# Linear attention into a SwiGLU block: turning phi(q) by 128x128 transposes instead of making phi on turned q, for one batch

## Chip, cores, metric

One core of a Trainium2 chip. The metric is the device time of one run in microseconds (us). "The stage" is a stretch from the first layer-2 matmul of the first token group to the first matmul of line L292 in the second group (its third block of layer 1; the first two blocks are line L276): it holds everything that the change touches.

## The reference, cut to what matters

```python
def phi(x):
    return np.where(x > 0, x, np.exp(x) - 1.0) + 1.0
q_p, k_p = phi(q), phi(k)                      # (8, 8, 576, 64)
kv  = einsum('bhsd,bhse->bhde', k_p, v)        # 64x64 per head
z   = k_p.sum(axis=2)
out = einsum('bhsd,bhde->bhse', q_p, kv) / (einsum('bhsd,bhd->bhs', q_p, z) + 1e-6)
x   = out, tokens x (heads*64)                 # 4608 x 512
y   = (silu(x @ w_gate) * (x @ w_val)) @ w_out # d_ff = 1536
```

With fp16 data the kernel computes phi as max(x, 0) + min(exp(x), 1), which is the same function.

## The kernel before: the parts concerned

The work goes in nine groups of 512 tokens. Per group, layer 1 is 12 blocks of 8 matmuls, layer 2 is 48 matmuls of 512 columns. The attention of the next tokens is woven in between. q and k lie with tokens on the partitions; the attention matmuls need phi(q) with the feature on the partitions, so q must be turned. For batch 1 this is done inside layer 2 of group 0:

```python
def qtr(b, lp, ps):                    # 16 transposes of 64 columns, raw q
    pt = ps[:, :].bitcast(FP16).rearrange("p (j c) -> p j c", c=P)
    for j in range(J - 1):
        for l2 in range(2):
            nc.tensor.transpose(out=pt[D * l2:D * l2 + D, j, :], in_=qr[b][:, 2 * lp + l2, D * j:D * j + D],
                                identity=id16[:, :])
# ... qtr8: 8 more, for column block 8 of batches 0 and 1
def t_phi(a, ps):                      # phi on turned q, out of PSUM
    return (lambda: act(a, ps, AF.Exp),
            lambda: nc.vector.tensor_scalar(out=a, in0=a, scalar1=1.0, scalar2=None, op0=ALU.min),
            lambda: nc.vector.scalar_tensor_tensor(out=a, in0=ps, scalar=0.0, in1=a, op0=ALU.max, op1=ALU.add))
# ...
    step = {1: [s0], 4: [s1, s3], 5: [s5]}    # what is done before which layer-2 block
    FO = 9
    for fb in range(FO):
        for f in step.get(fb, []):
            f()
        for t in range(4):
            l2_mm(0, t, fb)
    s4()                                      # the denominators of group 1
# ... three more blocks, numerators, then layer 1 of group 1
```

## Time and profile before

| | before |
|---|---|
| device time, median of 3 | 315.97 us (315.6 to 316.2) |
| span of the profiled run | 314.1 us |
| TensorE busy | 307.5 us, 98% |
| the stage | 36.75 to 54.88 us: 18.13 us |
| in it, to the first denominator matmul | 9.48 us |

The views used are the page (busy shares, chain that ended last), the chain in order of time (start, length, engine, tile, line), the waits (who waited for whom: total, times, longest), groups of instructions by form (busy time and mean ns, then idle time before them), and the timeline (start, length, engine, line, operation, count). On the timeline a length includes the last matmul's own 0.2 to 0.4 us; to get a pace one subtracts that. PE is TensorE, PEld its weight loads, DVE VectorE, ACT ScalarE, POOL GpSimd. The form of a matmul is the label that the views print behind it: 128*128 for layer 2 and the full-width transposes, 128*64 for the half-width ones, 64*64 for the denominators; a change of form is the step from one label to another.

### The profile page before, as it was taken

Reading aid. Unit: us, or ns where it says so; the run is one execution under the profiler, and the core shown is the slowest. Engines: PE = TensorE matmul, PEld = TensorE weight load, DVE = VectorE, ACT = ScalarE, POOL = GpSimd, SP = SyncE. Lnnn points to the kernel's source line nnn. Section 1 sums busy time; section 2 is a strip of 40 time slices with the busy share of each in tenths; the row PEclk is TensorE's granted clock in tenths of the full one; section 3 lists DMA queues with packets and bytes.
Section 4 is the critical chain, followed back from the end, with each engine's and each line's share of the span. In section 5 each row is a group of like instructions: output and inputs, shape, how many; then the busy total and the mean of one; then the engine's idle time right before and its main releaser. Section 6 shows DMA issues by size and latency. Waiting matters only on the chain.

```text
span 314.1 us, 5531 instructions
## 1 busy us (share of the span) xinstructions
PE 307.5 (98%) x2186; PEld 142.7 (45%) x2186; DVE 205.5 (65%) x362; ACT 152.0 (48%) x231; POOL 48.0 (15%) x72
## 2 busy tenths in 40 slices
PE   8899999999999999999999999999999999999994
PEld 4444444444544454445444544444444444444442
DVE  4854688899789767977597849874991434133410
ACT  4865839738643745366535743475330333133311
POOL 7755334300000230023000500000000000000000
PEclk9999999999999999999999999999999999999999
DMA  8999999995612396129702990314032400140014
GB/s 216 198 198 199 206 207 232 238 206 88 140 33 41 50 180 170 38 41 163 197 20 57 134 230 0 75 35 102 0 61 59 91 1 1 37 98 0 2 33 100
DMA packets 41162, 32.80 MB, mean 104 GB/s; under 512 B 16432, under 2 KB 36144, under 8 KB 41136
## 3 DMA queue, kind: packets, MB, share of 16 engines
q0 software_dynamic: 20464, 18.29, 37.2%
q1 hardware_dynamic: 20592, 14.13, 18.6%
q8 instruction: 17, 0.28, 0.4%
q14 instruction: 9, 0.07, 0.1%
q10 hardware_dynamic: 80, 0.03, 0.0%
HBM read 37.75 MB, written 9.44 MB: 150 GB/s over the span
## 4 chain that ended last, share of the span: by engine, by line
PE 96%; DMA 1%; DVE 1%; ACT 1%; issue 0%
PE pp L292 57%; PE pp L299 30%; PE pp L276 2%; PE pp L254 2%; PE pp L185 2%; DMA q<-in_q_dram 1%; PE pp L124 1%; PE pp L430 1%; ACT qT L120 0%; ACT ek L120 0%; PE pp L371 0%; PE pp L396 0%; DVE kp L159 0%; PE pp L212 0%; DVE ek L147 0%; DVE osb L322 0%
## 5 line engine op out<-in xcount | busy, mean ns | idle before, releaser
L120 ACT ACTIVATE sil<-pp 128x512 f16<-128x512 f32 x108 | 63.4, 597 | 101.8 <-PE pp L292 100.9
L292 PE MATMUL pp<-xT,wg 128*128 128x512 f16 x416 | 106.8, 379 | 0.0
L292 PE MATMUL pp<-xT,wv 128*128 128x512 f16 x416 | 106.8, 379 | 0.0
L285 DVE SCALAR_TENSOR_TENSOR hT<-pp,sil 128x512 f16<-128x512 f32 x108 | 72.4, 682 | 49.0 <-PE pp L292 35.6
L299 PE MATMUL pp<-wo,hT 128*128 128x512 f16 (+2 forms) x444 | 97.2, 374 | 0.6 <-DVE osb L322 0.6
L299 PEld LDWEIGHTS <-hT 128*128 128x128 f16 x444 | 41.9, 98 | 49.7 <-issue 2.1
L292 PEld LDWEIGHTS <-wv 128*128 128x128 f16 x416 | 40.7, 98 | 49.1
L292 PEld LDWEIGHTS <-wg 128*128 128x128 f16 x416 | 40.7, 98 | 48.4
L322 DVE TENSOR_SCALAR osb<-pp 128x512 f32<-128x512 f32 (+1 forms) x19 | 12.9, 682 | 30.6 <-PE pp L299 26.2
L120 ACT ACTIVATE osb<-pp 128x512 f32<-128x512 f32 (+1 forms) x18 | 10.3, 573 | 34.8 <-PE pp L299 34.8
L120 ACT ACTIVATE ek<-kr 128x1152 f16<-128x1152 f16 x16 | 17.8, 1156 | 0.1
L120 ACT ACT_TABLE_LOAD x13 | 16.7, 1283 | 2.3 <-PE pp L292 2.1
L693 POOL COPY gate<-qT 128x1 f16<-128x1 f16 x4 | 1.3, 320 | 97.9 <-DVE hT L285 71.2
L229 DVE TENSOR_TENSOR qp<-qp,rden 128x1152 f16<-128x1152 f16 x12 | 16.2, 1347 | 0.0
L220 DVE TENSOR_REDUCE den<-prod 128x18 f32<-128x1152 f16 x12 | 16.1, 1344 | 0.0
L271 DVE TENSOR_SCALAR xT<-pp 128x512 f16<-128x512 f32 (+1 forms) x14 | 8.8, 667 | 7.1 <-PE pp L254 7.1
L120 ACT ACTIVATE eq<-qr 128x1152 f16<-128x1152 f16 x12 | 13.2, 1147 | 0.0
L103 POOL DMA_DIRECT2D vr<-in_v_dram x16 | 11.7, 735 | 9.3 <-PE pp L292 3.5
L103 POOL DMA_DIRECT2D kr<-in_k_dram x16 | 11.7, 735 | 7.8 <-DMA wo<-in_moe_w_out_dram 1.8
L147 DVE TENSOR_SCALAR ek<-ek 128x1152 f16<-128x1152 f16 x16 | 7.7, 483 | 7.5 <-ACT ek L120 7.5
L159 DVE TENSOR_TENSOR kp<-ek,kp 128x1152 f16<-128x1152 f16 x16 | 12.1, 758 | 0.5
L103 POOL DMA_DIRECT2D qr<-in_q_dram x14 | 10.1, 723 | 5.8 <-DMA wo<-in_moe_w_out_dram 1.8
(76 smaller groups left out, 183.6 us busy)
## 6 DMA issues: line engine op xcount, KB each, us to landing
out_dram<-osb SPq DMA_DIRECT2D x70, 128.0 KB, 3.2
kr<-in_k_dram POOLq DMA_DIRECT2D x16, 288.0 KB, 8.9
vr<-in_v_dram POOLq DMA_DIRECT2D x16, 288.0 KB, 9.8
qr<-in_q_dram POOLq DMA_DIRECT2D x14, 288.0 KB, 12.1
wo<-in_moe_w_out_dram POOLq DMA_DIRECT2D x3, 512.0 KB, 12.7
wg<-in_moe_w_gate_dram POOLq DMA_DIRECT2D x5, 256.0 KB, 9.1
wv<-in_moe_w_val_dram POOLq DMA_DIRECT2D x5, 256.0 KB, 9.7
q<-in_q_dram SPq DMA_DIRECT2D x2, 576.0 KB, 4.1
```

The lines of the kernel that those rows point to most:

```text
L103: nc.gpsimd.dma_start(out=dst[b % NB][:, 2 * lp:2 * lp + 2, :], in_=src[b].rearrange("(l a) (c j) d -> (a c) l (j d)", a=2, j=J)[:, 2 * lp ...
L120: nc.scalar.activation(out=out, in_=in_, func=func, bias=bias, scale=scale)
L147: nc.vector.tensor_scalar(out=a, in0=a, scalar1=1.0, scalar2=None, op0=ALU.min)
L159: nc.vector.tensor_tensor(out=a, in0=ek[b % 2][:, lp, :, :], in1=a, op=ALU.add)
L185: nc.tensor.matmul(out=ps[hh][D * l2:D * l2 + D, D * lp:D * lp + D], lhsT=t[b % 2][rows, lp, j, D * l2:D * l2 + D], rhs=vr[b % NB][rows, 2 ...
L220: nc.vector.tensor_reduce(out=den[:, c, :], in_=prod[:, :, :].rearrange("p j (l d) -> p (j l) d", d=D), axis=AX.X, op=ALU.add)
L229: nc.vector.tensor_tensor(out=qv, in0=qv, in1=rden[:, c, :].unsqueeze(2).to_broadcast([P, 2 * J, D]), op=ALU.mult)
L271: nc.vector.tensor_scalar(out=dst, in0=ps[l2][:, c0:], scalar1=1.0 / SC, scalar2=None, op0=ALU.mult)
L285: nc.vector.scalar_tensor_tensor(out=hT[g % 2][:, fb, :], in0=ps[1][:, :], scalar=SC, in1=s[:, :], op0=ALU.mult, op1=ALU.mult)
L292: nc.tensor.matmul(out=ps[h][:, :], lhsT=w[:, c, P * fb:P * fb + P], rhs=xT[g % 2][:, c, :], start=(c == 0), stop=(c == 3))
L299: nc.tensor.matmul(out=l2p[(g, t)][:, n0:n1], lhsT=hT[g % 2][:, fb, P * t:P * t + P], rhs=wo[:, fb, n0:n1], start=(fb == 0), stop=(fb == F ...
L322: nc.vector.tensor_scalar(out=o[:, n0:n1], in0=ps[:, n0:n1], scalar1=1.0 / SC, scalar2=None, op0=ALU.mult)
```

## The change

Its intent is to halve the transposes (20 full-width ones in place of 40 half-width ones), and to take phi's work on PSUM off VectorE: phi(q) is made in the given layout out of SBUF, turned, and copied by ScalarE. To give VectorE room, half of the z sum goes to TensorE as nine 2-column matmuls.

```diff
-    def qtr(b, lp, ps):
+    def turn(lp, ps):
         pt = ps[:, :].bitcast(FP16).rearrange("p (j c) -> p j c", c=P)
         for j in range(J - 1):
-            for l2 in range(2):
-                nc.tensor.transpose(out=pt[D * l2:D * l2 + D, j, :], in_=qr[b][:, 2 * lp + l2, D * j:D * j + D],
-                                    identity=id16[:, :])
+            nc.tensor.transpose(out=pt[:, j, :], in_=qp[1][:, lp, j, :], identity=id16[:, :])
+        act(qT[1][:, lp, 0:8, :, :].rearrange("p j h c -> p (j h c)"), ps[:, :].bitcast(FP16))
 # ... mx_p, add_p: max and add of phi in the given layout; phi_q8: the same for block 8 of batch 0
 # ... turn8, copy8: block 8, one transpose per half, copied by VectorE
     def p1_z():
-        for lp in range(2):
-            ps = b1p["z"][1]
-            nc.tensor.matmul(out=ps[:, 2 * lp:2 * lp + 2], lhsT=zs[:, lp, 0, :], rhs=ob[:, 0:P:C],
-                             start=True, stop=True)
+        ps = b1p["z"][1]
+        nc.tensor.matmul(out=ps[:, 0:2], lhsT=zs[:, 0, 0, :], rhs=ob[:, 0:P:C], start=True, stop=True)
+        for j in range(J):
+            nc.tensor.matmul(out=ps[:, 2:4], lhsT=kp[1][:, 1, j, :], rhs=ob[:, 0:P:C],
+                             start=(j == 0), stop=(j == J - 1))
 # ...
         def s0():
-            qtr(1, 0, cq[0])
+            act(eq[0][:, :, D * 8:D * 9], qr[0][:, :, D * 8:D * 9], AF.Exp)
             exp_k(1, 1)
-            pm[0][0]()
+            exp_q(1, 0)
+            exp_q(1, 1)
+            phi_q8()
+            mx_p(0)
             mn_k(1, 1)
             add_k(1, 1)
-            zsum(1, 1, 2)
 # ...
+            mn_q(1, 0)
+            add_p(0)
+            mx_p(1)
+            mn_q(1, 1)
+            add_p(1)
         def s1():
# ... the old bodies of s1, s3 and s5 are left out
+            turn(0, cq[0])
         def s3():
+            turn(1, cq[1])
+            for b in range(2):
+                for lp in range(2):
+                    turn8(b, lp, dz[0])
             p1_z()
+            for b in range(2):
+                copy8(b, dz[0])
-        step = {1: [s0], 4: [s1, s3], 5: [s5]}
+        step = {1: [s0], 6: [s1], 8: [s3]}
```

More of the change, by code (lines that the diff above doesn't have):

```diff
@@ L363 @@
         nc.vector.memset(ob[C * h:C * h + C, C * h:C * h + C], 1.0)
-    def qtr(b, lp, ps):
+    def turn(lp, ps):
         pt = ps[:, :].bitcast(FP16).rearrange("p (j c) -> p j c", c=P)
         for j in range(J - 1):
-            for l2 in range(2):
-                nc.tensor.transpose(out=pt[D * l2:D * l2 + D, j, :], in_=qr[b][:, 2 * lp + l2, D * j:D * j + D],
-                                    identity=id16[:, :])
-    def qtr8(ps):
-        pt = ps[:, :].bitcast(FP16).rearrange("p (b i c) -> p b i c", i=4, c=P)
-        for b in range(2):
-            for lp in range(2):
-                for l2 in range(2):
-                    nc.tensor.transpose(out=pt[D * l2:D * l2 + D, b, lp, :],
-                                        in_=qr[b][:, 2 * lp + l2, D * 8:D * 9], identity=id16[:, :])
@@ L382, in t_phi @@
-    def t_phi(a, ps):
-        return (lambda: act(a, ps, AF.Exp),
-                lambda: nc.vector.tensor_scalar(out=a, in0=a, scalar1=1.0, scalar2=None, op0=ALU.min),
-                lambda: nc.vector.scalar_tensor_tensor(out=a, in0=ps, scalar=0.0, in1=a, op0=ALU.max, op1=ALU.add))
-    def t_phi_main(b, lp, ps):
-        return t_phi(qT[b][:, lp, 0:8, :, :].rearrange("p j h c -> p (j h c)"), ps[:, :].bitcast(FP16))
-    def t_phi_8(b, ps):
-        return t_phi(qT[b][:, :, 8, :, :].rearrange("p l h c -> p l (h c)"),
-                     ps[:, 256 * b:256 * b + P].bitcast(FP16).rearrange("p (l c) -> p l c", l=2))
+            nc.tensor.transpose(out=pt[:, j, :], in_=qp[1][:, lp, j, :], identity=id16[:, :])
@@ new lines, in turn, with mx_p, add_p, turn8 @@
+        act(qT[1][:, lp, 0:8, :, :].rearrange("p j h c -> p (j h c)"), ps[:, :].bitcast(FP16))
+    def mx_p(lp):
+        nc.vector.tensor_scalar(out=jl(qp, 1, lp), in0=lj(qr, 1, lp), scalar1=0.0, scalar2=None, op0=ALU.max)
+    def add_p(lp):
+        nc.vector.tensor_tensor(out=jl(qp, 1, lp), in0=jl(qp, 1, lp),
+                                in1=eq[1][:, hs(lp), :].rearrange("p l (j d) -> p l j d", d=D), op=ALU.add)
+    def turn8(b, lp, ps):
+        pt = ps[:, :].bitcast(FP16).rearrange("p (b i c) -> p b i c", i=4, c=P)
+        nc.tensor.transpose(out=pt[:, b, lp, :], in_=qp[b][:, lp, 8, :], identity=id16[:, :])
@@ new lines, in copy8, with phi_q8 @@
+    def copy8(b, ps):
+        nc.vector.tensor_copy(out=qT[b][:, :, 8, :, :].rearrange("p l h c -> p l (h c)"),
+                              in_=ps[:, 256 * b:256 * b + P].bitcast(FP16).rearrange("p (l c) -> p l c", l=2))
+    def phi_q8():
+        r, e = qr[0][:, :, D * 8:D * 9], eq[0][:, :, D * 8:D * 9]
+        nc.vector.tensor_scalar(out=r, in0=r, scalar1=0.0, scalar2=None, op0=ALU.max)
+        nc.vector.tensor_scalar(out=e, in0=e, scalar1=1.0, scalar2=None, op0=ALU.min)
+        nc.vector.tensor_tensor(out=qp[0][:, :, 8, :].rearrange("p a (l d) -> p a l d", d=D),
+                                in0=e.rearrange("p (a l) d -> p a l d", l=2),
+                                in1=r.rearrange("p (a l) d -> p a l d", l=2), op=ALU.add)
@@ L524, in p1_z @@
     def p1_z():
-        for lp in range(2):
-            ps = b1p["z"][1]
-            nc.tensor.matmul(out=ps[:, 2 * lp:2 * lp + 2], lhsT=zs[:, lp, 0, :], rhs=ob[:, 0:P:C],
-                             start=True, stop=True)
+        ps = b1p["z"][1]
[3 more added lines that the diff above has]
+                             start=(j == 0), stop=(j == J - 1))
         nc.vector.tensor_scalar(out=Zr[1][:, :, :, :].rearrange("p l h e -> p (l h) e"),
@@ L580, in layer2_0 @@
         cq, dz = b1p["q"], b1p["z"]
-        p8 = [t_phi_8(b, dz[0]) for b in range(2)]
-        pm = [t_phi_main(1, lp, cq[lp]) for lp in range(2)]
         nc.scalar.preload_act_table_set("natural_log_exp_and_others")
@@ L593, in s0 @@
         def s0():
-            qtr(1, 0, cq[0])
+            act(eq[0][:, :, D * 8:D * 9], qr[0][:, :, D * 8:D * 9], AF.Exp)
             exp_k(1, 1)
-            pm[0][0]()
+            exp_q(1, 0)
+            exp_q(1, 1)
+            phi_q8()
+            mx_p(0)
             mn_k(1, 1)
             add_k(1, 1)
-            zsum(1, 1, 2)
-            pm[0][1]()
-            pm[0][2]()
+            mn_q(1, 0)
[3 more added lines that the diff above has]
+            add_p(1)
         def s1():
-            qtr8(dz[0])
-            for f in (0, 1, 2):
-                for b in range(2):
-                    p8[b][f]()
+            turn(0, cq[0])
         def s3():
-            qtr(1, 1, cq[1])
-            pm[1][0]()
-        def s5():
+            turn(1, cq[1])
+            for b in range(2):
+                for lp in range(2):
+                    turn8(b, lp, dz[0])
             p1_z()
-            pm[1][1]()
-            pm[1][2]()
+            for b in range(2):
+                copy8(b, dz[0])
         def s4():
```

## The prediction

> **What bounds the kernel now.** I read the page of the kernel before from the top: busy shares first, then the 40 slices (the granted TensorE clock is 9 tenths or more in all of them, so nothing is to be won by warming), then the chain that ended last.
>
> ```profile
> PE 307.5 (98%) x2186; PEld 142.7 (45%) x2186; DVE 205.5 (65%) x362; ACT 152.0 (48%) x231; POOL 48.0 (15%) x72
> ...
> PE 96%; DMA 1%; DVE 1%; ACT 1%; issue 0%
> ```
>
> TensorE sets the end. Only 6.6 us of the 314.1 us span have no matmul in them, so removed VectorE or ScalarE work is worth nothing unless TensorE waited for it. The change touches only batch 1, whose preparation is woven into layer 2 of the first group. So I next read the chain in order of time there (columns: start, length, engine, tile, source line, count):
>
> ```profile
> 36.91 0.86 PE pp L299 x4
> 37.77 0.57 PE pp L371 x16
> 38.34 2.70 PE pp L299 x12
> 41.04 0.34 PE pp L379 x8
> 41.38 0.45 PE pp L371 x16
> 41.83 0.97 PE pp L299 x4
> 42.80 0.03 PE pp L527 x2
> 42.83 3.48 PE pp L299 x16
> 46.30 0.69 PE pp L254 x16
> ```
>
> The chain never leaves TensorE here. L299 is layer 2, L371 and L379 are the 40 transposes of raw q, L527 sums z, L254 is where the denominators start. From 36.91 to 46.30 is 9.39 us. Layer 2 at its usual pace takes 36 x 0.2155 = 7.76 us (0.2155: sixteen in 3.48 us less the switch, and 96 in 20.72 us elsewhere). The other 1.63 us is everything the change can touch on TensorE. The wait view of that stretch shows what stood idle:
>
> ```profile
> ACT lnt L120 <- PE pp L254: 3.7, 1, 3.7
> ...
> ACT qT L120 <- PE pp L379: 1.4, 1, 1.4
> ```
>
> ScalarE waits for TensorE, never the reverse; it has over 5 us to spare before the denominators. VectorE is busy 8.1 of 9.4 us in that stretch, with little spare. The groups by form give the durations that I use:
>
> ```profile
> L120 ACT ACTIVATE eq<-qr 128x1152 f16<-128x1152 f16 x2 | 2.2, 1147 | 0.0
> L385 DVE SCALAR_TENSOR_TENSOR qT<-pp,qT 128x1024 f16<-128x1024 f16 x2 | 2.5, 1225 | 0.1
> L159 DVE TENSOR_TENSOR kp<-ek,kp 128x1152 f16<-128x1152 f16 x3 | 2.3, 759 | 0.1
> L147 DVE TENSOR_SCALAR ek<-ek 128x1152 f16<-128x1152 f16 x3 | 1.4, 454 | 1.0 <-ACT ek L120 1.0
> L120 ACT ACTIVATE qT<-pp 128x1024 f16<-128x1024 f16 x2 | 2.0, 1018 | 0.0
> L371 PE MATMUL pp<-id,qr 128*64 128x128 f16 x32 | 1.3, 220 | 0.0
> L529 DVE TENSOR_SCALAR Zr<-pp 128x256 f16<-128x256 f32 x1 | 0.4, 416 | 0.0
> ```
>
> [...] nine 2-column matmuls for z early on (0.38 us for nine, of which 0.166 is one matmul's own length) step at (0.38 - 0.17)/8 = 27 ns. [...] the old transposes have the form 128*64, [...]and sixteen take 0.64 us of which 0.22 is one, so they step at 0.42/15 = 28 ns[...]; and the surrounding pieces are longer than their counts by about 0.11 us at each change of form (2.70 us against 12 x 0.2155 = 2.59; 0.97 against 0.86; 0.57 against 16 x 0.028 = 0.45; 0.34 against 0.22). [...] here a copy from PSUM of 1024 should thus cost as exp did, 1018 ns.
>
> **The change, part by part.**
> TensorE. Removed: 40 half-width transposes at 28 ns (1.12 us), four changes of form (4 x 0.115 = 0.46 us), two z matmuls (0.05 us): 1.63 us, the whole of the remainder above. Added: [...]no change of form, since layer 2 is 128*128 too, and ten z matmuls at 28 ns (0.28 us): 1.40 us. Halving the count of transposes thus saves nothing in streaming: the old ones ran in pairs. Net -0.23 us, from switches saved less z moved in.
>
> VectorE. Removed: two min of 1024 (0.52 each), two max-add from PSUM (1.23 each), their small forms (2 x 0.22, 2 x 0.42), and one z sum of four steps (0.43+0.29+0.22+0.22 = 1.16): 5.9 us. Added: two max (0.45), two min (0.45), two add (0.76), the three small ones for column block 8 of batch 0 (0.22+0.22+0.29), two copies from PSUM of 256 (0.42 each, estimated as like the 416 ns row): 4.9 us. One us less, but it isn't on the path.
>
> ScalarE. Removed: exp on PSUM, 2 x 1.02 + 2 x 0.38 = 2.8 us. Added: exp of 2 x 1.15 + 0.42, copies 2 x 1.02: 4.8 us. Two us more, into idle time.
>
> What matters is whether the new order makes TensorE wait. The start of ScalarE's part in this stage:
>
> ```profile
> 36.70 1.28 ACT L583 ACT_TABLE_LOAD   x1
> ...
> 37.18 0.45 DVE L143 TENSOR_SCALAR kp<-kr 128x1152 f16<-128x1152 f16 x1
> 37.54 0.69 DVE L285 SCALAR_TENSOR_TENSOR hT<-pp,sil 128x512 f16<-128x512 f32 x1
> ```
>
> ScalarE from 37.99: small exp to 38.4, exp of k to 39.45, exp of q to 40.5 and 41.5 (they step at 1.05, as two took 2.20). VectorE from 38.2: small max, min, add to 38.95; max of q to 39.3; min of k (after 39.45) to 39.95, add to 40.75; min of q to 41.1, add to 41.9; second max to 42.3, min to 42.6, add to 43.4.
>
> TensorE reaches the first turn after 24 layer-2 matmuls: 36.75 + 24 x 0.2155 = 41.92. phi(q) of the first half is ready at 41.9 plus some 0.05 of hand-over: **a wait of 0.05 to 0.2 us**, say 0.1. Turn over at 42.45. Eight more bring the second turn to 44.2, with its input at 43.4: no wait. It ends at 44.65, the four last transposes at 44.85, z at 45.15, four layer-2 matmuls at 46.0. ScalarE's second copy is done by 45.8, in time.
>
> VectorE starts the Zr broadcast when the last z matmul has drained, 45.15 + 0.15, and does Zr to 45.7, copies of block 8 to 46.05 and 46.4 (overlapping by 0.08 each). The denominators' first four matmuls need the first copy; the next ones write over the same PSUM bank that the second copy still reads. So TensorE, there at 46.0, **waits until about 46.4**, with four small matmuls done in between, where before it began at 46.23. In the old order those small phi steps sat before Zr and were long done. The rest of that stage (logs, exp, xT, layer 1 from 51.3) hangs on this point and moves with it.
>
> Sum: -0.23 (TensorE work) + 0.1 (first turn) + 0.3 (denominators, 0.4 less what the four matmuls fill) = **+0.2 us**. Predicted 316.1 us.
>
> **Rivals.**
> (a) No waits: VectorE and ScalarE run slightly ahead and the copies are shorter. Then -0.23 us, 315.7. For it: both waits are under half a microsecond, and each hangs on a sum of ten durations. Against it: two VectorE copies now follow z inside 0.9 us of cover, and they need 1.25.
> [...]
> (c) A transfer decides. Layer 2 now starts its later blocks earlier, and the weights and q of batch 1 are still landing. The queue's waits put the second block of w_out at 38.4 and the third at 42.4; TensorE would need them at 36.75 + 16 x 0.2155 = 40.2 and at 45.1. The second half of q lands about 39.9 and is now wanted by exp at 40.4 rather than by a transpose at 41.2. Half a us of slack; if it is missed the last exp slides, but its add has 0.8 us before the second turn. Worth 0 to +0.3 us.
> (d) ScalarE or VectorE becomes the bound of the stage: ScalarE's load there rises to about 6.7 of 9.4 us, VectorE's falls to about 7: no.
>
> **Range and chances.** [...] the runs before spread by 0.6 us. Range **315.3 to 316.9**. 2% is 6.3 us, more than four times all work of this change on TensorE, so within 2% is near certain: faster 0.01, same 0.98, slower 0.01.
>
> **What would show it.** In the profile after: 20 transposes of form 128*128, eight in about 0.45 us, with no longer pieces of layer 2 beside them; TensorE's sum over the stage about 0.2 us less; a short TensorE wait on VectorE's qp before the first turn; a TensorE wait on VectorE's qT copy of 0.2 to 0.4 us before the denominators; ScalarE's copies near 1.02 us; everything from layer 1 of the second group on the same, shifted by 0 to 0.5 us. I am wrong in a step [...] if the first turn waits over 0.5 us (a transfer or a slow VectorE step), or if TensorE doesn't wait before the denominators. A change over 2 us either way would mean a mechanism that I haven't seen.

Terms are cut out of this text. Its sum came to +0.2 us (-0.23 + 0.1 + 0.3, 316.1 us), and the -0.23 is 1.40 us of new work on TensorE less 1.63 us of old. Of the 1.40 us, 0.28 stand above; the other 1.12 us were the 20 full-width transposes, whose pace was an estimate that was not taken from the trace. The run gives the same sum: they step at 56 ns (after: eight in 0.61 us less 0.22 for one, over seven), and 20 x 0.056 is 1.12 us. That the half-width ones "ran in pairs" also lacks its support above; half_width shows it below (28 ns each, half of those 56).

## The result, and the profile after

The changed kernel took 315.33 us (median of 4 runs, 315.24 to 316.28), the kernel before 316.06 us beside it (median of 4, 315.6 to 316.2). The ratio is 0.9986, with a 95% interval of 0.9964 to 1.0008: the same. The predicted time was 316.1 us in a range of 315.3 to 316.9; the measured one lies at its lower edge.

The page of the kernel after, busy shares and the chain's engines:

```profile
PE 307.2 (98%) x2174; PEld 142.7 (46%) x2174; DVE 203.9 (65%) x361; ACT 153.9 (49%) x232; POOL 47.0 (15%) x72
...
PE 94%; DVE 2%; ACT 2%; DMA 1%; issue 0%
```

TensorE sets the end as before, but now the chain leaves it for 4% of the span in favour of VectorE and ScalarE, against 2% before. The chain in order of time shows where that happens:

```profile
40.22 0.58 DVE eq L155
...
40.82 0.77 DVE qp L377
...
41.64 0.62 PE pp L370 x8
42.26 1.73 PE pp L299 x8
43.98 0.45 PE pp L370 x8
44.43 0.22 PE pp L382 x4
...
44.90 0.89 PE pp L299 x4
...
45.81 0.64 PE pp L254 x16
```

The first turn (L370) hung on the addition that ends the first half of phi(q) on VectorE (L377). Layer-2 pieces beside the turns have no excess any more: 1.73 us for 8 matmuls is 8 x 0.2155. Eight transposes take 0.45 us and four take 0.22: 56 ns each. The waits of the same stretch and three groups by form:

```profile
PEld L370 <- DVE qp L377: 0.6, 1, 0.6
```

```profile
L120 ACT ACTIVATE qT<-pp 128x1024 f16<-128x1024 f16 x2 | 2.0, 1024 | 2.4 <-PE pp L370 2.4
...
L155 DVE TENSOR_SCALAR eq<-eq 128x1152 f16<-128x1152 f16 x2 | 1.1, 554 | 0.0
...
L385 DVE COPY qT<-pp 128x256 f16<-128x256 f16 x2 | 0.5, 278 | 0.0
```

The 0.6 us is the idle time of the weight-load path; TensorE itself began the turn at 41.64 us, where 36.21 + 24 x 0.2155 = 41.38 had been possible, so 0.26 us were lost. ScalarE's copies are as long as exp was (1024 ns). One of VectorE's two min operations (L155) was stretched: 554 ns on average against 450 elsewhere; on the timeline the first took 0.65 us. The copies of block 8 (L385) took 278 ns, where I had put 420.

So the stage took 54.33 - 36.21 = 18.12 us, against 18.13 before. And yet the span is 0.5 us shorter. The reason lies before any changed instruction, in the first sixteen transposes of batch 0's q. The timeline of TensorE, of before and then of after:

```profile
4.86 1.37 PE L430 MATMUL pp<-id,qr 128*64 128x128 f16 x16 [0.21 <-DVE qr L448]
```

```profile
4.85 0.89 PE L432 MATMUL pp<-id,qr 128*64 128x128 f16 x16 [0.30 <-DVE qr L450]
```

Same instructions, same start, 1.37 against 0.89 us; the stage then began at 36.75 in one and at 36.21 in the other. Whether that is chance or comes with the change had to be tested.

### The profile page after: what moved, and what is told of

It reads as the page before. It is cut to its first block, busy times and chain, and to the rows that moved or that the text cites. A ratio compares the mean times of both kernels' runs of the same rounds, so it can differ in the third digit from the quotient of the medians.

```text
span 313.6 us, 5504 instructions
## 1 busy us (share of the span) xinstructions
PE 307.2 (98%) x2174; PEld 142.7 (46%) x2174; DVE 203.9 (65%) x361; ACT 153.9 (49%) x232; POOL 47.0 (15%) x72
## 3 DMA queue, kind: packets, MB, share of 16 engines
HBM read 37.75 MB, written 9.44 MB: 150 GB/s over the span
## 4 chain that ended last, share of the span: by engine, by line
PE 94%; DVE 2%; ACT 2%; DMA 1%; issue 0%
PE pp L292 57%; PE pp L299 29%; PE pp L276 2%; PE pp L254 2%; PE pp L185 2%; DMA q<-in_q_dram 1%; PE pp L124 1%; PE pp L432 1%; DVE kp L159 0%; ACT L584 0%; ACT qT L120 0%; PE pp L370 0%; ACT ek L120 0%; DVE ek L147 0%; PE pp L398 0%; DVE qp L377 0%
## 5 line engine op out<-in xcount | busy, mean ns | idle before, releaser
L299 PE MATMUL pp<-wo,hT 128*128 128x512 f16 (+2 forms) x444 | 97.1, 373 | 0.7 <-DVE osb L322 0.7
L299 PEld LDWEIGHTS <-hT 128*128 128x128 f16 x444 | 42.0, 98 | 49.8 <-issue 2.1
L120 ACT ACTIVATE eq<-qr 128x1152 f16<-128x1152 f16 (+1 forms) x15 | 15.8, 1098 | 0.0
```

The source lines that it names most:

```text
L120: nc.scalar.activation(out=out, in_=in_, func=func, bias=bias, scale=scale)
L299: nc.tensor.matmul(out=l2p[(g, t)][:, n0:n1], lhsT=hT[g % 2][:, fb, P * t:P * t + P], rhs=wo[:, fb, n0:n1], start=(fb == 0), stop=(fb == F ...
```

## The experiments

Theory: the change is worth nothing to about a tenth of a us (less work on TensorE, paid back in two short waits for VectorE), and the rest of the measured difference is the start. Rival A: the whole 0.7 us belong to the change. Rival B: halving the transposes saved TensorE much, and something else took it back. Rival C: the waits are not waits but costs of TensorE going over to other work.

All eleven runs gave correct results. "Whole run" is the median; with one run it says little, as runs of one kernel spread by about a us.

| run | stage starts | to denominators | stage | whole run (before beside it) |
|---|---|---|---|---|
| before, first profile | 36.75 | 9.48 | 18.13 | |
| after, first profile | 36.21 | 9.60 | 18.12 | 315.33 (316.06) |
| before_again | 36.25 | 9.49 | 18.01 | 315.51 (315.60) |
| after_again | 36.21 | 9.44 | 17.96 | 315.60 (315.60) |
| half_width | 36.26 | 9.90 | 18.41 | 315.59, one run |
| z_alone | 36.45 | 9.70 | 18.21 | 315.64, one run |
| turn_later | 36.45 | 9.34 | 17.86 | 315.14, one run |
| z_back | 36.27 | 9.29 | 17.81 | 314.86, one run |
| copies_early | 36.58 | 9.45 | 17.97 | 315.49, one run |
| both_moves | 37.04 | 9.25 | 17.77 | 315.13 (315.57) |
| all_moves | 36.50 | 9.26 | 17.77 | 315.27 (315.68) |
| all_moves_2 | 36.73 | 9.03 | 17.55 | 314.93 (315.75) |
| no_warm | 38.09 | 9.39 | 17.91 | 316.92, one run |

### before_again and after_again: both kernels unchanged

No edit. What was expected:

> The kernel before, unchanged, against itself. Both theories expect a ratio of 1 within 0.2%. What it tells apart: the profile of the kernel after reaches its first layer-2 matmul at 36.21 us and that of before at 36.75 us, before any changed instruction has run. If that 0.54 us is chance (the first sixteen transposes of q run slow or fast in either kernel[...]), the runs of this kernel should also spread over about 0.5 to 1 us and its profile may show the first layer-2 matmul at either time. If it belongs to the change (another program length), this profile shows 36.75 again and its runs stay near 316.0.

> The changed kernel, unchanged, for a closer interval. Measured by the stage alone (from the first layer-2 matmul of the first group to the first layer-1 matmul of the second group's third block), the two kernels took 18.13 and 18.12 us, so theory one (the change is worth nothing to 0.1 us; the rest is the start) expects a ratio of 0.999 to 1.001 with some runs near 315.3 and some near 316.2. The rival (the change is worth 0.6 us) expects 0.998 and every run near 315.3.

Measured: before against itself 1.0005 (0.9992 to 1.0019), runs from 315.06 to 316.39 us; after against before 1.0004 (0.9990 to 1.0017), runs from 315.13 to 316.42 us. This time the profile of before has the fast start: its sixteen transposes took 0.89 us and its stage began at 36.25 us. So the start doesn't belong to the change, and rival A falls. (Both profiles of the changed kernel have the fast start; its variants, alike up to there, show 0.96 to 1.47 us in six of seven.) In the stage the second pair differs by 0.05 us, the first by 0.01.

It also shows something that I had missed in before. Its stage was 18.13 us in the first profile and 18.01 in the second. VectorE's timeline before the denominators, in the first profile:

```profile
44.66 0.62 DVE L384 TENSOR_SCALAR qT<-qT 128x1024 f16<-128x1024 f16 x1
45.30 1.23 DVE L385 SCALAR_TENSOR_TENSOR qT<-pp,qT 128x1024 f16<-128x1024 f16 x1
```

and in the second:

```profile
44.16 0.42 DVE L384 TENSOR_SCALAR qT<-qT 128x1024 f16<-128x1024 f16 x1
44.61 1.22 DVE L385 SCALAR_TENSOR_TENSOR qT<-pp,qT 128x1024 f16<-128x1024 f16 x1
```

In the first, the last max-add of phi ended at 46.53 us, 0.30 us after TensorE had begun the denominators (46.23), and their sixteen matmuls took 0.69 us until layer 2 went on. In the second it ended at 45.83, 0.09 after they began (45.74), and they took 0.57. TensorE's weight loads in the first profile show the wait itself: eleven of sixteen went through, and the other five came 0.06 us after the max-add's end, where in the second profile all sixteen ran in one row.

```profile
46.23 0.17 PEld L254 LDWEIGHTS <-Zr 64*64 64x64 f16 x11 [0.42 <-issue]
46.59 0.14 PEld L254 LDWEIGHTS <-Zr 64*64 64x64 f16 x5 [0.18 <-issue]
```

The kernel before thus stood on the edge of a wait for VectorE, and a min that took 0.20 us longer pushed it over.

### half_width: the old form of transpose, all else as after

```diff
-            nc.tensor.transpose(out=pt[:, j, :], in_=qp[1][:, lp, j, :], identity=id16[:, :])
+            for l2 in range(2):
+                nc.tensor.transpose(out=pt[D * l2:D * l2 + D, j, :], in_=qp[1][:, lp, j, D * l2:D * l2 + D],
+                                    identity=id16[:, :])
```

and the same in turn8.

> The changed kernel with its 20 full-width transposes taken as 40 half-width ones of the old form on the same phi(q), nothing else altered. Theory: half-width ones run in pairs, so streaming costs the same (16 in about 0.45 us), and only the four changes of form come back, about 0.11 us each. The first two fall partly into the wait for phi(q), so the stage grows by 0.25 to 0.45 us, to 18.4 to 18.6. Rival one (fewer instructions are cheaper: a transpose costs its issue) expects sixteen in about 0.9 us and a stage longer by 1 us or more. Rival two (no cost of changing form) expects 18.1.

Measured: TensorE's timeline:

```profile
41.63 0.64 PE L371 MATMUL pp<-id,qp 128*64 128x128 f16 x16
42.20 1.90 PE L299 MATMUL pp<-wo,hT 128*128 128x512 f16 x8
44.03 0.64 PE L371 MATMUL pp<-id,qp 128*64 128x128 f16 x16
```

The sixteen half-width transposes take 0.64 us less 0.22 for one: 28 ns each, so the eight pairs of them stream as long as the eight full ones. What came back is the change of form. From the first turn to layer 2 is 0.57 us (42.20 - 41.63) against 0.46 in after_again (41.94 - 41.48): one change, 0.11 us. From there to the end of z it is 2.90 us (45.10 - 42.20) against 2.66 (44.60 - 41.94): two changes, 0.12 each. The fourth lies before the first turn, where TensorE waits for phi(q) anyway; there the stage lost 0.10 us more than in after_again, because the addition that ends the first half of phi(q) on VectorE came that much later (its end is 5.32 us after the start of the stage, against 5.21; a min before it took 0.61 us). So of the 0.45 us by which this stage is longer than that of after_again, 0.35 are three changes of form and 0.10 a late phi(q). Both rivals of this run fall.

### z_alone: the kernel before with only the z part

```diff
-            zsum(1, 1, 2)
```

in s0 of the kernel before, and p1_z as in the change.

> The kernel before with one part of the change: the second half of the z sum made by nine 2-column matmuls instead of four VectorE additions. In the trace of before, the last max-add of phi on VectorE ended at 46.53 us, after TensorE had come to the denominators at 46.23, and their sixteen matmuls took 0.69 us, against 0.57 in the changed kernel. Theory (a short hidden wait of some 0.12 us on VectorE there): TensorE gets 0.22 us more work, VectorE 1.2 us less, the max-add ends before the denominators start and they take about 0.57 us, so the stage is 0.1 us longer than 18.13. Rival (no wait there): 0.22 us longer, with the denominators at 0.69 us still.

Measured: the stage was 18.21 us, 0.08 longer than the first profile of before and 0.20 longer than the second; the denominators took 0.56 us. Against the first profile that is the theory's 0.1 us with 0.57; but the second profile has the 0.57 as well without the z part. So the run shows what z costs on TensorE (0.2 us for eight more matmuls), and that with VectorE relieved the wait is absent, but not that z is what removed it: it was absent in before_again too.

### turn_later: the first turn one block later

```diff
-        step = {1: [s0], 6: [s1], 8: [s3]}
+        step = {1: [s0], 7: [s1], 8: [s3]}
```

> The changed kernel with the first turn one block of layer 2 (four matmuls, 0.86 us) later, nothing else. Theory: phi(q) of the first half comes 0.1 us (second look at the changed kernel) to 0.26 us (first look) after TensorE wants it; one block later it is there, so the load before the first turn waits for nothing, and the stage (first layer-2 matmul to the layer-1 matmuls of the third block) shrinks from 17.96 to 18.12 us to about 17.86. Rival (the time before the turn is a cost of TensorE going over to transposes, not a wait): the gap stays and so does the stage.

Measured: 17.86 us, as expected; in TensorE's timeline the 28 layer-2 matmuls and the turn stand without a gap (36.45 + 28 x 0.2155 = 42.48):

```profile
42.49 0.61 PE L370 MATMUL pp<-id,qp 128*128 128x128 f16 x8
```

The time before the first turn was a wait for phi(q), 0.10 us in one look at the changed kernel and 0.26 in the other. Rival C falls for it.

### z_back: the second half of z back on VectorE

```diff
-        for j in range(J):
-            nc.tensor.matmul(out=ps[:, 2:4], lhsT=kp[1][:, 1, j, :], ...)
+        nc.tensor.matmul(out=ps[:, 2:4], lhsT=zs[:, 1, 0, :], rhs=ob[:, 0:P:C], start=True, stop=True)
 # s0, at its end, after add_p(1)
+            zsum(1, 1, 2)
```

> The changed kernel with the second half of the z sum back on VectorE, as four additions after the last addition of phi(q), and one 2-column matmul instead of nine. Theory: eight matmuls of about 27 ns leave TensorE (-0.22 us) and VectorE ends its additions about 44.1 us after the start, 0.2 us before TensorE wants z, so the stage is 0.2 us shorter, near 17.75 to 17.9. Rival (VectorE is too full, which was the reason to move it): TensorE waits for z and the gain is lost or turned into 0.2 us or more of loss.

Measured: 17.81 us. VectorE's last addition of z ended at 44.26 us and TensorE's first z matmul ran at 44.46, unhindered. Moving z to TensorE was thus no gain in this place: VectorE had the time for it after phi(q), and TensorE paid 0.2 us. (The stage is only 0.15 us shorter than in after_again, as the first turn waited 0.17 us here, 41.61 - 36.27 - 5.17, and 0.10 there.)

### copies_early: z and batch 0's block 8 one block earlier

```diff
+        def s2():
+            p1_z()
+            for lp in range(2):
+                turn8(0, lp, dz[0])
+            copy8(0, dz[0])
         def s3():
             turn(1, cq[1])
-            for b in range(2):
-                for lp in range(2):
-                    turn8(b, lp, dz[0])
-            p1_z()
-            for b in range(2):
-                copy8(b, dz[0])
+            for lp in range(2):
+                turn8(1, lp, dz[0])
+            copy8(1, dz[0])
-        step = {1: [s0], 6: [s1], 8: [s3]}
+        step = {1: [s0], 6: [s1], 7: [s2], 8: [s3]}
```

> The changed kernel with z, the two transposes of batch 0's block 8 and their copy put one block of layer 2 earlier; only batch 1's block 8 and its copy stay behind the second turn. Theory: the 0.10 us that TensorE still waits for VectorE's copies before the denominators (1.05 us from the last block's first matmul, of which 0.86 is the block and 0.09 the change of form) goes; it becomes 0.95, and the stage is 0.1 us shorter. Rival (that tenth is all change of form): it stays 1.05.

Measured: TensorE's timeline:

```profile
45.08 1.02 PE L299 MATMUL pp<-wo,hT 128*128 128x512 f16 x4
46.03 0.64 PE L254 MATMUL pp<-qT,Zr 64*64 64x64 f16 x16
```

From the last block's first matmul to the denominators it is 0.95 us (46.03 - 45.08) against 1.05 in both profiles of after (45.81 - 44.76), so 0.10 us had been the wait for the copies. The other 0.09 us stays with no copy near (this one ended at 45.57), and stands in the kernel before too; I call it the change of form. The stage was 17.97 us, no shorter than in after_again, because the wait before the first turn was 0.21 us this time (41.96 - 36.58 - 5.17): one of VectorE's max operations took 0.70 us instead of 0.45.

### both_moves: the two moves together

```diff
-        step = {1: [s0], 6: [s1], 7: [s2], 8: [s3]}
+        step = {1: [s0], 7: [s1, s2], 8: [s3]}
```

on copies_early.

> The two moves together: first turn one block later, and z and block 8 of batch 0 right behind it. Theory: both waits go, TensorE does its 36 layer-2 matmuls (7.76 us), 20 transposes and ten z matmuls (1.39 us) and one change of form (0.09 us): 9.24 us to the denominators against 9.44 to 9.60 in the changed kernel and 9.48 to 9.49 before; the stage is 17.75 to 17.85 us. The whole run gains 0.2 to 0.35 us, under the spread of half a microsecond that the start of the kernel gives: ratio 0.998 to 1.000. Rival (waits move on to the next hand-over, ScalarE's copy of the first turn): the denominators start no earlier.

Measured: 9.25 us to the denominators and a stage of 17.77, as worked out. The whole run: 0.9983 (0.9969 to 0.9996).

### all_moves: z back on VectorE as well

On both_moves: p1_z and zsum as in z_back, p1_z back behind the second turn with copy8(1) before it.

> The changed kernel with the first turn one block later, batch 0's block 8 right behind it, batch 1's block 8 copied before z, and the second half of z back on VectorE (four additions after phi(q), one 2-column matmul). Theory: TensorE has 36 layer-2 matmuls (7.76 us), 20 transposes (1.12), two z matmuls (0.06) and one change of form (0.09), with no waits: 9.03 to 9.1 us to the denominators, and a stage of 17.5 to 17.6 us against 18.0 to 18.1 before. The whole run gains 0.45 to 0.55 us: ratio 0.9983 give or take the spread of the start. Rival (VectorE's additions end too late for z): a TensorE wait of 0.2 us or more before z, stage 17.75 or more, no better than the two moves without it.

Measured: a miss. The stage was 17.77 us, as without z's move, which is the number of the rival but not for its reason. TensorE did not wait for z, but for something that I had overlooked. Its timeline, and VectorE's:

```profile
43.97 0.61 PE L370 MATMUL pp<-id,qp 128*128 128x128 f16 x8
44.64 0.27 PE L382 MATMUL pp<-id,qp 128*128 128x128 f16 x2
```

```profile
44.30 0.28 DVE L385 COPY qT<-pp 128x256 f16<-128x256 f16 x1
```

The turn was over at 44.42 (43.97 + 8 x 0.056), and batch 1's block 8 began at 44.64, just after VectorE had copied batch 0's block 8 out of the same PSUM tile (44.58). The copy was in VectorE's queue behind z's additions. The two blocks lie in different columns of the tile; the wait is there all the same, 0.22 us (44.64 - 44.42). Whole run: 0.9983 (0.9965 to 1.0002).

### all_moves_2: that copy out of VectorE's queue

```diff
-            copy8(0, dz[0])
+            act(qT[0][:, :, 8, :, :].rearrange("p l h c -> p l (h c)"),
+                dz[0][:, 0:P].bitcast(FP16).rearrange("p (l c) -> p l c", l=2))
-        step = {1: [s0], 7: [s1, s2], 8: [s3]}
+        step = {1: [s0], 6: [s2], 7: [s1], 8: [s3]}
```

> As all_moves, but the two transposes of batch 0's block 8 come before the first turn and their copy goes to ScalarE, which is idle then. In all_moves the second pair of block 8 waited 0.22 us for VectorE's copy of the first pair, which stood behind z's additions and reads the same PSUM tile. Theory: with that copy out of VectorE's queue no wait is left; the denominators start 9.03 to 9.1 us after the first layer-2 matmul and the stage is 17.5 to 17.6 us. Rival (the 0.22 us belong to z's additions, which TensorE then waits for before z): 9.25 us and 17.75 again. Over the whole run 0.998 to 0.999 either way, as the start spreads by more than that.

Measured: 9.03 us to the denominators, 17.55 us for the stage: what TensorE's own work adds up to. In its timeline nothing is missing between the turn, the two transposes and layer 2:

```profile
44.20 0.61 PE L370 MATMUL pp<-id,qp 128*128 128x128 f16 x8
44.64 0.27 PE L382 MATMUL pp<-id,qp 128*128 128x128 f16 x2
```

The whole run is 314.93 us (median of 5, 314.75 to 315.32) against 315.75 beside it: 0.9970 (0.9956 to 0.9984), clear of 1 but by the 2% rule the same. The stage accounts for 0.46 to 0.58 us of it (18.01 and 18.13 less 17.55); the rest of the measured 0.8 us is within what the start can do (36.21 to 37.04 us among the profiles but no_warm's), which is not shown for these runs.

### no_warm: what makes the start vary

```diff
-    WARM = (4, 3, 4, 4, 2, 1, 2, 2)
+    WARM = (0, 3, 4, 4, 2, 1, 2, 2)
```

> The changed kernel without its first four warm-up matmuls (they start 1.06 us into the run and use constants only). It asks what makes the start vary by half a microsecond: in ten profiles so far the first sixteen transposes of q took 0.89 to 1.47 us and the layer-2 stage began at 36.21 to 37.04 us, later with the slower ones. Theory (TensorE still runs at half pace then[...]): without those matmuls it is busy for a shorter time before, so the sixteen take 1.3 us or more and the stage begins at 36.8 us or later. Rival (something else, such as the arrival of q): nothing changes, the sixteen take 0.9 us in most cases and the stage begins near 36.3.

Measured: TensorE's timeline, and one stretch of the windows view (busy time per engine, then the granted clock, here 1.00, and DMA):

```profile
4.95 1.49 PE L432 MATMUL pp<-id,qr 128*64 128x128 f16 x16 [1.86 <-DVE qr L450]
6.38 1.46 PE L124 MATMUL pp<-ones 128*128 128x512 f16 x3
```

```profile
6.00:7.00 1.00, 1.00 (x8) 0.48 (x5) 0.97 (x3) 0.92 (x2) 1.00 (x2) 1.00 1.16 192
```

The sixteen took 1.49 us, hardly more than the 1.47 of both_moves; but the three 512-column matmuls after them took 1.46 us, against 0.82 in each of the twelve other profiles, and the stage began at 38.09 us. The q of batch 0 came no later than elsewhere (4.95 us; 4.79 to 5.02 in the others), so the rival falls. The run took 316.92 us. So, as far as one run can show it, the pace at the start does hang on those four matmuls. Half pace at the start, which the theory takes for granted, can be read where the warm-up itself was looked at (before, after, all_moves, all_moves_2): its four matmuls step at 0.42 us (1.06 to 2.74 us), against 0.2155 later. By what rule the pace rises is not shown. Nor is what makes the sixteen differ, 0.89 to 1.47 us across the twelve other profiles, all with the same warm-up.

## Why the prediction was right, and where it was off

- **TensorE's work** (-0.23 us, 1.63 to 1.40): right. In after_again, 9.44 us to the denominators less 36 x 0.2155, less 0.10 and 0.10 of waits and 0.09 of the last change of form, leaves 1.39 us. The old transposes did run in pairs, and the saving is in the changes of form (half_width, three visible ones at 0.11 to 0.12 us). The full-width ones step at 56 ns (0.61 us for eight, less 0.22 for one, over seven). That pace need not have been left to an estimate: at the end of before, twelve load-and-multiply pairs of 128 columns (L299, from 309.80 us, 0.83 us in all) step at (0.83 - 0.22)/11 = 56 ns.
- **VectorE and ScalarE off the path**: right in sum. In the 9.4 us up to the first denominator matmul (46.23 us before, 45.81 in the first profile of after) VectorE's busy time fell from 8.13 to 7.16 us and ScalarE's rose from 4.80 to 6.66, the one us less and two more of the prediction; the time followed neither sum, only the moment at which single results came.
- **First turn, +0.1 us, between 0.05 and 0.2**: 0.26 and 0.10 in the two profiles, 0.21 in copies_early. The order was right; that a 0.45 us operation can take 0.65 was not in the sum, and 0.26 lies outside its range. The stretching is nearly all of the spread: without it the wait is 0.04 to 0.06 us (0.26 - 0.20, 0.10 - 0.06; half_width 0.20 - 0.16, z_back 0.17 - 0.11), the hand-over that was predicted. When an operation is stretched is told in the last point of this document.
- **Before the denominators, +0.3 us**: this term was mis-sized. It was 0.10 us (copies_early). The step that failed is "two copies from PSUM of 256 (0.42 each, estimated as like the 416 ns row)": that row reads fp32, the copies read fp16 and took 0.278 us, stepping at 0.20 (no run shows whether the type is the reason). I had both copies done 1.25 us after the last z matmul; in the first profile of after it was 1.0 us (44.76 to 45.75), against 0.86 us of layer 2 as cover. And 0.09 us of the change of form, which comes anyway, lay inside what I had counted as waiting. Nor were "four small matmuls" done in between: all sixteen began at 45.81, 0.06 us after the second copy's end, and ran as fast as elsewhere (0.57 us).
- **"ScalarE waits for TensorE, never the reverse"** held, but the kernel before was not free of waits for VectorE either: in its first profile the denominators took 0.12 us longer for a late max-add. I read no wait in the view because it lists this one as "issue" of the weight loads. In the order of the change those phi steps end near 43.1 us, and no profile of it shows that wait.
- **"Nothing is to be won by warming"**: a wrong reading. The granted clock reads 1.00 in before from 1 us on, while the warm-up matmuls step at half pace (0.42 us), so that view can't tell; the start moved the stage by 0.83 us between profiles, more than all the terms of the sum together.
- **Rivals (a) and (c)**: (a), no waits, came near: the copies were shorter and the waits smaller, but both were there. (c), a transfer, didn't come: in turn_later nothing holds the layer-2 matmuls from 36.45 us to the last block's start at 44.74, so the pieces of w_out were there.
- **The sum, +0.2 us**: -0.01 and -0.05 us in the two pairs of profiles. With the denominators' term at 0.10 it is -0.23 + 0.10 + 0.10 = -0.03 for after_again; for the first profile -0.23 + 0.26 + 0.10 = +0.13 to the denominators (measured +0.12), less the 0.12 that before lost after that point.
- **The time itself**: 316.1 predicted, 315.33 and 315.60 measured, and before's own median moved from 315.97 to 315.60. The range held it, at the edge, but that is luck: the stages of the first two profiles differ by 0.01 us and their starts by 0.54, and the prediction didn't treat the start. What can be credited to it is the "same" and the two waits, found where it had put them.

## What to carry to other kernels

Two half-width transposes into different halves of the partitions already take the time of one full-width transpose (28 ns each against 56), so merging them into one saves nothing per column; what it saves is the change of form beside 128x128 work, 0.11 to 0.12 us each here. On an engine that sets the end, such a gain is easily handed back by a producer that comes a tenth of a us late (the first turn waited 0.10 and 0.26 us, and one block later not at all), so place each hand-over one block later than the sum says, and keep reads and writes of one PSUM tile from queueing behind unrelated work (0.22 us in all_moves). And when a change is smaller than the spread of whole runs, measure its stage inside the trace and run the old kernel against itself first.

## What else the traces show

- Load-and-multiply pairs in a row step at 56 ns with 128 columns (eight transposes: 0.61 us less 0.22, over seven; twelve matmuls of 128 columns at the end of before) and at 215.5 ns with 512 (layer 2).
- Each 128x128 transpose is recorded with a length of 220 ns (after, 16 of them), though they step at 56 ns.
- A change of form cost 0.11 to 0.12 us each (half_width, three of them, 0.35 us).
- The granted clock read 1.00 where 512-column matmuls ran at about half pace (no_warm: three in 1.46 us, against 0.82; before and after: a step of 0.42 us from 1.06 us on, against 0.2155 later), so the spacing of the matmuls is what to read.
- Ten max and min operations of the stage on VectorE, in the 13 profiles, were stretched by 0.04 to 0.25 us, and each began 0.27 to 0.48 us after a GpSimd DMA issue (0.71 us long) had begun: the later, the less (0.27: 0.25; 0.33: 0.20; 0.42: 0.11; 0.48: 0.04), so that begin and stretch add up to about 0.52 us into the issue, not to its end. None that began at another time was (first profile of after: issue from 38.39 us, max from 38.51 for 0.46). In three cases it was the issue that was longer: the operation began 0.22 to 0.27 us into it and took 0.45 us, and the issue took 0.82 to 0.86. The spread of the first turn's wait comes from these stretched operations; no run moved an issue, so what stretches them is not shown.
